# Query lots looked at one by one in the ring, six query sums in the long burst, and a two-input epsilon

## The chip, the cores and the metric

One Trainium2 chip, one core. The number that counts is device time in microseconds for one execution. The kernel before takes 1162.13 us (median of 3 runs, 1161.17 to 1162.33).

## The reference, cut to what matters

Agent attention, then a feed-forward layer with a cosine gate. 4 batches of 12480 tokens with 128 channels, 49 agents for each batch, float32 throughout.

```python
def sm(a, b):                                   # scaled, shifted softmax
    s = (a @ b.T) / sqrt(128)
    e = exp(s - s.max(-1))
    return e / (e.sum(-1) + 1e-9)
agent_v = sm(agents, k) @ v                     # 49 x 128 for each batch
x = sm(q, agents) @ agent_v                     # one row for each token
h = x @ w_in                                    # 2048 wide
out = (h * cos(h)) @ w_out
```

## The kernel before

Tokens are worked on in 52 query lots (NQ) of 960 tokens, 13 for each batch, laid out as 120 partitions x 8 rows (GT). For a lot the query weights are a 120 x 8 x 49 array: scores against the agents (TensorE), minus the maximum over 49 (a reduction and a subtraction), exponential (ScalarE), sum over 49, plus epsilon, reciprocal (VectorE), product with the reciprocal (GpSimd), transposition (TensorE) and a split into two parts (GpSimd).

The main loop has 832 steps, 16 for each lot (8 pairs of w_in columns x 2 halves of the lot). A step issues two matmuls `ph`, one ScalarE cosine `c`, one VectorE instruction `r` (the cosine minus one, times h), and, four steps later (LAG), two matmuls `po` that accumulate the output. The `ph` tiles come from a ring of three PSUM tiles of two banks each (ps_h): the matmuls of step n+3 wait until VectorE has read the tile of step n. There is one more PSUM tile for everything small (`one`) and one for the accumulator `po`.

Everything else is laid into these steps by two lists, `plan` (work ahead of the VectorE instruction of its step) and `post` (work behind it). Each engine runs its instructions in program order, so an instruction that waits holds up all behind it on its engine. Among this work are the next batch's key scores and running maximum (`scores`, `rank`), the split of its exponentials and values for TensorE (`split`, on GpSimd), its sums (`values`), and the query lots.

Sine and exponential are in different ScalarE tables, so exponentials are done in bursts (`burst`), with a table load ahead and behind. `pieces` lists the lots whose exponentials share a burst. There are three kinds:

- the long burst, at step 112 of batches 0 to 2 (T1): the key exponentials of the next batch in three parts, then the exponentials of six query lots. The scores of four further lots are made here too, two at a time, by two calls of `query_two`, each in one ring tile, one bank for each lot.
- the short bursts, at step 26 and at step 8 of batches 1 to 3: the exponentials of six or seven query lots, and one `query_two`.
- a last one of four lots at step 96 of batch 3, without `query_two`.

Behind its exponentials, a long burst sums the first SF lots on VectorE (`query_sum`), adds epsilon and takes the reciprocals (`query_inverse`), all in its own step. From four steps later (SM) it sums the others one in a step, and one step after the last sum adds epsilon and takes the reciprocals again. In the other bursts three lots are summed on VectorE (SD1) and the rest on GpSimd (`query_sums`).

`query_inverse` adds epsilon by `tensor_scalar_add` (EP = 0); the branch for EP = 1 is there already: `scalar_tensor_tensor(rz, rz, EPS, rz, op0=add, op1=max)`, which takes the maximum of rz + epsilon and rz. `rank` starts the running maximum of each batch by `tensor_copy`. All recorded instructions go through one wrapper, so the profile gives line 182 for nearly all; they are told apart by their tiles.

Of the kernel before, what the change touches and what calls it, by code (L numbers as in the profile page):

```python
# [9 lines left out]
F32 = mybir.dt.float32  # L10
# [5 lines left out]
AX = mybir.AxisListType  # L16
# [3 lines left out]
TT = 120  # L20
GT = 8
# [24 lines left out]
SH = 1  # L46
AD = 2
KB = 24
SF = 3
ST = 4  # L50
SD0 = 2
SD1 = 3
# [50 lines left out]
PO = 14  # L103
PK = 0
BM = 38
EP = 0
BZ = 12
TS = 1
VX = [5, 6, 7, 8]
# [35 lines left out]
def agent_attention_cos_ffn(ctx, tc, qT, kT, v, agT, w_in, w_out, outT):  # L145
    nc = tc.nc
    NB, _, N = qT.shape
    NA = agT.shape[2]
# [39 lines left out]
    pe, dve, act, pool = (Ordered(x) for x in (nc.tensor, nc.vector, nc.scalar, nc.gpsimd))  # L188
# [25 lines left out]
    def load(dst, src):  # L214
        ins = nc.sync.dma_start(dst, src)
        if pinned[0]:
            tc.keep_in_program_order(ins)

    def twice(x):

        return x.unsqueeze(1).to_broadcast([x.shape[0], 2, NA])
# [89 lines left out]
    class Agents:  # L311
# [50 lines left out]
        def rank(self, g):  # L362
            self.ranks = g + 1
            if g == 0:
                dve.tensor_copy(self.run, self.part(g))
            else:
                dve.tensor_max(self.run, self.run, self.part(g))

# [247 lines left out]
    with ExitStack() as pools:  # L616
        sb = pools.enter_context(tc.tile_pool(name="sb", bufs=2))
# [8 lines left out]
        def pair():  # L626
            return ps_h.tile([P, 2, 512], F32, name="ph")
# [4 lines left out]
        a = []  # L632
# [25 lines left out]
        e_of, rz_of = {}, {}  # L658
# [41 lines left out]
        def query_two(two, piece):  # L700

            ps = pair()[:TT]
            for j, n in enumerate(two):
                xt = sb.tile([P, GRP], F32, name="xt", bufs=XT)
                load(xt, qT[n // NG, :, n % NG * GRP:(n % NG + 1) * GRP])
                for t in range(GT):
                    pe.matmul(ps[:, j, t * NA:(t + 2) * NA].rearrange("p (x a) -> p x a", x=2) if WB else ps[:, j, t * NA:(t + 1) * NA],
                              xt[:, t * TT:(t + 1) * TT], twice(ag[:, n // NG, :]) if WB else ag[:, n // NG, :], start=True, stop=True)
            ps = ps[:, :, :GT * NA].rearrange("p j (t a) -> p j t a", a=NA)
            mx = sb.tile([TT, 2, GT], F32, name="mx3", bufs=2)  # L710
            dve.reduce_max(mx, ps, axis=AX.X)
            room(piece)
            i = piece.index(two[0])
            dve.tensor_sub(whole[piece][:, i * GT:(i + 2) * GT].rearrange("p (j t) a -> p j t a", j=2), ps,
                           mx.unsqueeze(3).to_broadcast([TT, 2, GT, NA]))

        whole = {}

        def room(piece):
            if piece in whole:  # L720
                return
            if OG and piece == pieces[-1]:
                e = ab[-1].s[:, :len(piece) * GT]
                rz = sb.tile([TT, len(piece) * GT], F32, name="rz3", bufs=1)
            else:
                e = sb.tile([P, PIECES * GT, NA], F32, name="e", bufs=EB)[:TT]
                rz = sb.tile([TT, PIECES * GT], F32, name="rz2", bufs=EB)
            whole[piece] = e
            for i, k in enumerate(piece):
                e_of[k], rz_of[k] = e[:, i * GT:(i + 1) * GT], rz[:, i * GT:(i + 1) * GT]  # L730
            e_of[piece], rz_of[piece] = e[:, :len(piece) * GT], rz[:, :len(piece) * GT]
# [22 lines left out]
        def query_inverse(piece, i, j):  # L754
            rz = rz_of[piece][:, i * GT:j * GT]
            if EP:
                dve.scalar_tensor_tensor(rz, rz, EPS, rz, op0=ALU.add, op1=ALU.max)
# [139 lines left out]
        piece = pieces[0]  # L897
# [11 lines left out]
        for g in range(NG):  # L909
# [6 lines left out]
            ps = pair()  # L916
# [88 lines left out]
        plan, post = Plan(), Plan()  # L1005
# [25 lines left out]
        def burst(n, piece, two=(), ab=None, also=()):  # L1031

            shut.update(range(n, n + SHUT))
            wide_at.update(range(n, n + SHUT + WX))
            for i in range(0, len(two), 2):
                post(n + i // 2 * BD, query_two, two[i:i + 2], piece_of[two[0]])
            if ab is not None:
                for g, k in lots:
                    post(n, pinned_exp, ab, g, k)
            post(n, query_exp, piece)  # L1040
            if also:
                post(n, query_exp, also)
                post(n + 12, query_sums, also, 0, len(also))
                post(n + 20, query_inverse, also, 0, len(also))
            s0 = SF if ab is not None else SD1
            for k in piece[:s0]:
                post(n, query_sum, k)
            post(n, query_inverse, piece, 0, s0)
            m = n + SM
            if ab is not None:  # L1050
                for k in piece[s0:]:
                    post(m, query_sum, k)
                    m += 1
                post(m, query_inverse, piece, s0, len(piece))
                return
            for i in range(s0, len(piece), ST):
                j = min(i + ST, len(piece))
                post(m, query_sums, piece, i, j)
                m += 1
            post(m + (SR if n < T3 + (NB - 1) * PER else SZ), query_inverse, piece, s0, len(piece))  # L1060
# [20 lines left out]
        late = [pieces[2 * b + 3] for b in range(NB - 1)] + [()]  # L1081
        spread_over(SA, S0 - SD, S0 - SD, [q_lot(n) for n in pieces[1]])
        burst(S0 + 2, pieces[1], early[0][:N0])
        for b in range(NB):
            o = b * PER
# [9 lines left out]
            if b == NB - 1:  # L1095
                spread_over(k0, go - 5, go - 1, [q_lot(n) for n in early[b][N2:]])
                burst(go, early[b])
                for c in range(DFF // 512):
                    if BZ >> c & 1:
                        post(go, big_late)  # L1100
                for i in range(FB):
                    post(go + FO, keep_warm)
                break
# [11 lines left out]
            for g in range(NG):  # L1115
                plan(k1 + 16 + SH * g, nxt.shift, g, 1, pool)
            burst(go, early[b], late[b][:N1], nxt)
            for g in range(0, NG, VP):
                at = go + V0 + (o + V1 - go - V0) * g / NG
# [7 lines left out]
            i = (b + 1) % 2  # L1127
# [11 lines left out]
        while queue or begun:  # L1139
# [4 lines left out]
            x = min(ready, key=lambda x: (x[2], x[1]))  # L1144
            if x is not begun:
                queue.remove(x)
            n, i, by, parts = x
# [17 lines left out]
        for n in range(NSTEP + LAG):  # L1165
# [3 lines left out]
            if n < NSTEP:  # L1169
                q, c, i = n // STEP, n // NP % NCH, n % NP  # L1170
# [31 lines left out]
            m = n - LAG  # L1202
            if m < 0:
                continue
            q, c, i = m // STEP, m // NP % NCH, m % NP
# [41 lines left out]
    with tc.If(far):  # L1247
        with ExitStack() as pools:
            sb = pools.enter_context(tc.tile_pool(name="gsb", bufs=2))
# [8 lines left out]
            p = sb.tile([TT, HT, 2 * HI], F32, name="p", bufs=1)  # L1258
# [121 lines left out]
```

## Time and profile before

| | |
|---|---|
| time of the runs shown | 1162.13 us, median (1161.17 to 1162.33) |
| the profiled execution | 1160.97 us; its span, first to last instruction, 1159.2 us |
| granted TensorE clock | 0.998 over the span |
| busy, share of the span | PE 97%, DVE 92%, ACT 84%, POOL 49% |
| chain that ended last | PE 62%, DVE 21%, ACT 11%, issue 4%, POOL 1% |
| DVE: `r`, whole tiles | 808 instructions, 891.4 us |
| DVE: reductions over two lots, `mx` from `ph` | 10 instructions, 9.7 us |
| DVE: sums `rz` of one lot | 36 instructions, 18.3 us |
| DVE: epsilon, 24 elements | 13 instructions, 6.0 us |

PE is TensorE's matmuls, DVE is VectorE, ACT is ScalarE, POOL is GpSimd. A busy share is over the whole span; a burst is a few microseconds in which other engines bound the work than in the steps around it. The chain of waits follows back from the last instruction, at each step to what released it.

### The profile page before, as it was taken

What the parts mean: (1) busy time and instruction counts of PE and PEld (TensorE: products, weight loads), DVE (VectorE), ACT (ScalarE), POOL (GpSimd) and SP (SyncE); (2) the same over time, 40 slices, a digit from 0 to 9 for tenths busy, and PEclk for the clock granted to TensorE, in tenths of its full rate; (3) what the DMA queues carried; (4) which work ended last, traced back from release to release, by engine and by line L of the source; (5) the groups of instructions that cost most, each with busy time, mean ns of one, the idle gap of its engine ahead of it and who ended that gap; (6) DMA issues with size and microseconds to landing.
All of it is one profiled execution on the core that took longest, in us unless ns stands there. A gap on an engine that the chain in (4) does not pass through costs nothing.

```text
span 1159.2 us, 17231 instructions
## 1 busy us (share of the span) xinstructions
PE 1118.7 (97%) x6075; PEld 924.1 (80%) x6075; DVE 1064.4 (92%) x1201; ACT 977.2 (84%) x1268; POOL 564.2 (49%) x726
## 2 busy tenths in 40 slices
PE   9989999999999999999999999999999999999996
PEld 8869888878887888877887888887888777767774
DVE  5888989999998999989999999998999899999996
ACT  3568877889889888898888887888988999999996
POOL 2013313678964122559893331366896455535551
PEclk9999999999999999999999999999999999999999
DMA  8734342143332232233331332224331100000001
GB/s 331 308 141 136 104 130 92 57 148 101 99 106 68 85 103 86 86 104 106 107 108 53 110 96 86 86 68 139 108 107 52 35 18 35 34 18 35 18 35 38
DMA packets 31631, 109.44 MB, mean 94 GB/s; under 512 B 3504, under 2 KB 4016, under 8 KB 31536
## 3 DMA queue, kind: packets, MB, share of 16 engines
q1 hardware_dynamic: 31392, 108.13, 28.7%
q8 instruction: 50, 0.82, 0.3%
q14 instruction: 45, 0.37, 0.1%
q10 hardware_dynamic: 144, 0.12, 0.0%
HBM read 82.68 MB, written 25.56 MB: 93 GB/s over the span
## 4 chain that ended last, share of the span: by engine, by line
PE 62%; DVE 21%; ACT 11%; issue 4%; POOL 1%; DMA 0%; ACTq 0%; DVEq 0%
PE ph L182 27%; PE po L182 23%; DVE r L182 15%; PE one L182 12%; ACT c L182 6%; DVE rz L182 2%; ACT osb L182 2%; DVE e L182 1%; DVE mx L182 1%; ACT p L182 1%; DVE sums L182 1%; ACT s L182 1%; ACT e L182 1%; ACT L182 1%; DVE s L182 1%
## 5 line engine op out<-in xcount | busy, mean ns | idle before, releaser
L182 DVE SCALAR_TENSOR_TENSOR r<-c,ph 128x960 fp32r<-128x960 f32 (+1 forms) x833 | 907.4, 1132 | 49.1 <-ACT c L182 41.8
L182 ACT ACTIVATE c<-ph 128x960 f32<-128x960 f32 x832 | 783.5, 977 | 132.8 <-PE ph L182 122.5
L182 PE MATMUL ph<-pT,a 113*128 113x480 f32 x1664 | 517.1, 392 | 16.3 <-DVE r L182 12.6
L182 PE MATMUL po<-r,w 128*128 128x480 f32 x1664 | 523.8, 396 | 5.6 <-ACT osb L182 5.3
L182 PEld LDWEIGHTS ph<-pT,a 113*128 113x128 f32 x1664 | 296.7, 189 | 123.0 <-DVE r L182 60.9
L182 PEld LDWEIGHTS po<-r,w 128*128 128x128 f32 x1664 | 291.8, 189 | 52.7 <-ACT osb L182 14.8
L182 POOL CAST pT<-p 49x480 fp32r<-49x480 f32 x102 | 59.2, 580 | 282.6 <-ACT p L182 279.8
L182 PEld LDWEIGHTS one<-ag,xt 128*120 128x120 f32 x1088 | 134.7, 184 | 11.3 <-DVE sums L182 1.5
L182 PE MATMUL one<-ag,xt 128*120 128x98 f32 x1088 | 134.2, 265 | 0.7 <-DVE b L182 0.4
L182 POOL TENSOR_TENSOR pT<-p,pT 49x480 fp32r<-49x480 f32 x102 | 124.1, 1217 | 8.2
L182 POOL TENSOR_TENSOR vh<-vt,vh 120x512 fp32r<-120x512 f32 x78 | 93.3, 1196 | 30.6 <-ACT vh L182 30.6
L182 POOL TENSOR_TENSOR p<-e,rz 120x392 f32<-120x392 f32 x51 | 43.5, 853 | 48.1 <-DVE rz L182 47.0
L182 PE MATMUL po<-pT,b 113*128 113x480 f32 x208 | 62.4, 381 | 0.0
L182 POOL TENSOR_TENSOR raw<-c,raw 128x480 f32<-128x480 f32 x23 | 28.3, 1229 | 70.0 <-ACT raw L182 69.9
L182 ACT COPY osb<-po 128x480 f32<-128x480 f32 x104 | 58.1, 559 | 2.2 <-PE po L182 2.2
L182 PEld LDWEIGHTS ph<-ag,xt 128*120 128x120 f32 x480 | 53.1, 188 | 7.5 <-DVE r L182 4.4
L182 PE MATMUL ph<-ag,xt 128*120 128x98 f32 x480 | 55.4, 272 | 3.1 <-DVE r L182 2.0
L182 POOL TENSOR_TENSOR e<-e,mx 120x392 f32<-120x392 f32 x26 | 21.9, 843 | 71.0 <-DVE mx L182 71.0
L182 PEld LDWEIGHTS one<-vh,eh 120*113 120x113 f32 x312 | 45.9, 177 | 8.2 <-POOL vh L182 2.5
L182 PE MATMUL one<-vh,eh 120*113 120x258 f32 x312 | 50.7, 284 | 1.4 <-DVE e L182 0.9
L182 POOL TENSOR_TENSOR eh<-s,eh 120x196 fp32r<-120x196 f32 x78 | 47.6, 610 | 6.3
L182 PEld LDWEIGHTS po<-pT,b 113*128 113x128 f32 x208 | 38.8, 188 | 6.0
(137 smaller groups left out, 725.4 us busy)
## 6 DMA issues: line engine op xcount, KB each, us to landing
xt<-qT SPq DMA_DIRECT2D x52, 480.0 KB, 3.5
outT<-osb SPq DMA_DIRECT2D x51, 480.0 KB, 2.8
xt<-kT SPq DMA_DIRECT2D x46, 480.0 KB, 3.7
vt<-v SPq DMA_DIRECT2D x43, 512.0 KB, 3.7
c<-kT SPq DMA_DIRECT2D x6, 480.0 KB, 6.9
vh<-v SPq DMA_DIRECT2D x5, 512.0 KB, 6.6
raw<-w_in SPq DMA_DIRECT2D x2, 512.0 KB, 6.5
a<-w_in SPq DMA_DIRECT2D x2, 512.0 KB, 5.7
```

What stands on the lines that cost most here:

```text
L182: ins = f(*args, **kw)
```

## The change

Three settings and two functions. `SF` goes from 3 to 6, so in a long burst all six query lots are summed in the burst's own step, with one epsilon and one reciprocal instruction for the six; the four later posts (three sums, one inverse) are gone. `query_two` makes the scores of one lot, then the maximum and the difference of that lot, then those of the other; the tile is still one for both, a bank for each. `EP` goes from 0 to 1, and `rank` starts with `tensor_max` of the part with itself in place of a copy.

```diff
-SF = 3
+SF = 6
...
-EP = 0
+EP = 1
...
             if g == 0:
-                dve.tensor_copy(self.run, self.part(g))
+                dve.tensor_max(self.run, self.part(g), self.part(g))
...
                 for t in range(GT):
                     pe.matmul(ps[:, j, t * NA:(t + 2) * NA].rearrange("p (x a) -> p x a", x=2) if WB else ps[:, j, t * NA:(t + 1) * NA],
                               xt[:, t * TT:(t + 1) * TT], twice(ag[:, n // NG, :]) if WB else ag[:, n // NG, :], start=True, stop=True)
-            ps = ps[:, :, :GT * NA].rearrange("p j (t a) -> p j t a", a=NA)
-            mx = sb.tile([TT, 2, GT], F32, name="mx3", bufs=2)
-            dve.reduce_max(mx, ps, axis=AX.X)
-            room(piece)
-            i = piece.index(two[0])
-            dve.tensor_sub(whole[piece][:, i * GT:(i + 2) * GT].rearrange("p (j t) a -> p j t a", j=2), ps,
-                           mx.unsqueeze(3).to_broadcast([TT, 2, GT, NA]))
+                x = ps[:, j, :GT * NA].rearrange("p (t a) -> p t a", a=NA)
+                mx = sb.tile([TT, GT], F32, name="mx3", bufs=4)
+                dve.reduce_max(mx, x, axis=AX.X)
+                room(piece)
+                dve.tensor_sub(e_of[n], x, mx.unsqueeze(2).to_broadcast([TT, GT, NA]))
...
-                post(m, query_inverse, piece, s0, len(piece))
+                if s0 < len(piece):
+                    post(m, query_inverse, piece, s0, len(piece))
```

## Rows read from the trace of the kernel before

**Rows 1.** The page: busy time of each engine, share of the span, instructions.
```profile
PE 1118.7 (97%) x6075; PEld 924.1 (80%) x6075; DVE 1064.4 (92%) x1201; ACT 977.2 (84%) x1268; POOL 564.2 (49%) x726
```

**Rows 2.** Busy engines by stretch, second long burst: PE, PEld, DVE, ACT, POOL, clock, DMA.
```profile
516.00:529.00 13.00, 11.29 (x52) 7.47 (x51) 12.83 (x17) 10.33 (x14) 11.88 (x16) 1.00 0.53 156
529.00:566.00 37.00, 36.62 (x184) 30.39 (x183) 36.39 (x38) 33.41 (x41) 31.52 (x46) 1.00 0.30 89
```

**Rows 3.** Timeline of DVE, second long burst: start, length, operation, [idle before].
```profile
511.97 0.97 DVE L182 TENSOR_REDUCE mx<-ph 120x16 f32<-120x784 f32 x1 [1.66 <-PE ph L182]
...
513.87 1.49 DVE L182 TENSOR_REDUCE rz<-e 120x8 f32<-120x392 f32 x3
515.39 0.18 DVE L182 TENSOR_SCALAR rz<-rz 120x24 f32<-120x24 f32 x1
...
516.10 1.16 DVE L182 SCALAR_TENSOR_TENSOR r<-c,ph 128x960 fp32r<-128x960 f32 x1 [0.20 <-ACT c L182]
517.17 0.56 DVE L182 TENSOR_REDUCE mx<-one 120x8 f32<-120x392 f32 x1
...
518.25 3.27 DVE L182 SCALAR_TENSOR_TENSOR r<-c,ph 128x960 fp32r<-128x960 f32 x3
...
526.37 0.86 DVE L182 TENSOR_SCALAR rz<-rz 120x24 f32<-120x24 f32 x1
...
527.48 3.22 DVE L182 SCALAR_TENSOR_TENSOR r<-c,ph 128x960 fp32r<-128x960 f32 x3
```

**Rows 4.** Timeline of ACT, the same burst.
```profile
511.17 2.62 ACT L182 ACTIVATE e<-e 120x392 f32<-120x392 f32 x6
...
515.10 0.97 ACT L182 ACTIVATE c<-ph 128x960 f32<-128x960 f32 x1
```

**Rows 5.** Timeline of PE, the same burst.
```profile
528.63 0.70 PE L182 MATMUL ph<-pT,a 113*128 113x480 f32 x2 [0.49 <-DVE r L182]
```

**Rows 6.** Groups of DVE instructions by form: busy us, mean ns, idle before.
```profile
L182 DVE RECIPROCAL rz<-rz 120x24 f32<-120x24 f32 x13 | 3.9, 303 | 0.4
...
L182 DVE COPY run<-s 120x392 f32<-120x392 f32 x4 | 2.2, 538 | 7.4 <-ACT s L182 7.4
```

**Rows 7.** Timelines of PE, DVE and POOL, first long burst.
```profile
233.96 1.92 PE L182 MATMUL ph<-ag,xt 128*120 128x98 f32 x16 [0.69 <-DMA xt<-qT]
...
239.77 1.09 DVE L182 SCALAR_TENSOR_TENSOR r<-c,ph 128x960 fp32r<-128x960 f32 x1
...
240.04 1.20 POOL L182 TENSOR_TENSOR vh<-vt,vh 120x512 fp32r<-120x512 f32 x1 [7.42 <-ACT vh L182]
```

**Rows 8.** Timelines of PE, DVE, ACT and POOL, short burst of batch 1.
```profile
366.09 3.60 PE L182 MATMUL ph<-ag,xt 128*120 128x98 f32 x32 [0.36 <-DVE r L182]
...
375.62 0.70 PE L182 MATMUL ph<-pT,a 113*128 113x480 f32 x2 [0.70 <-DVE r L182]
...
373.22 1.00 DVE L182 TENSOR_SCALAR rz<-rz 120x24 f32<-120x24 f32 x1
...
372.41 1.83 ACT L182 ACTIVATE c<-ph 128x960 f32<-128x960 f32 x2
...
371.24 1.86 POOL L182 TENSOR_TENSOR raw<-e 120x768 f32<-120x768 f32 x1 [4.45 <-ACT e L182]
373.18 2.45 POOL L182 TENSOR_TENSOR raw<-raw 120x384 f32<-120x384 f32 x4
```

**Rows 9.** Timelines of DVE and POOL: a running maximum beside a GpSimd product.
```profile
395.46 0.66 DVE L182 TENSOR_TENSOR run<-run,s 120x392 f32<-120x392 f32 x1
...
394.85 0.84 POOL L182 TENSOR_TENSOR p<-e,rz 120x392 f32<-120x392 f32 x1
```

**Rows 10.** Timeline of DVE, last burst.
```profile
1025.07 1.50 DVE L182 TENSOR_REDUCE rz<-e 120x8 f32<-120x392 f32 x3 [0.45 <-ACT e L182]
...
1038.55 0.79 DVE L182 TENSOR_SCALAR rz<-rz 120x8 f32<-120x8 f32 x1
```

**Rows 11.** Timeline of ACT, last burst.
```profile
1024.51 1.79 ACT L182 ACTIVATE e<-e 120x392 f32<-120x392 f32 x4
```

## The prediction

> **What bounds the kernel now.** I read the page first: PE is busy 97% of the span, DVE 92%, ACT 84% [rows 1]. With three engines this close an average says little, so I cut the span into stretches and looked around each burst. The stretch behind the second long burst stands apart: in 516 to 529 us DVE is busy 12.83 of 13 us and PE 11.29, while in the 37 us after it PE is busy 36.62 [rows 2]. So PE sets the pace nearly everywhere, and DVE does for some 13 us behind each of the three long bursts. The timeline of PE confirms it: its last idle time there, at 528.63, is ended by DVE's `r` [rows 5]. The chain of waits shows the same for some 10 us behind the short bursts of batches 1 and 2, where PE sits idle 0.70 us for `r` [rows 8]. Work taken off DVE is worth something in these stretches, up to PE's idle time in them, and nearly nothing elsewhere.
>
> **Six sums in the long burst.** Removed behind each long burst: three single sums, one epsilon, one reciprocal. A sum costs DVE 0.47 us of pace: three in a row last 1.49, one of them 0.55 with its tail, so (1.49 - 0.55) / 2 [rows 3, 10]. Three are 1.41. From the second epsilon to the next `r` it is 527.48 - 526.37 = 1.11 [rows 3]. Together 2.52 us.
>
> Added in the burst itself: `r` cannot start before the sums end. In the second burst the scores of the fourth lot are there at 511.97 [rows 3]. Looked at alone, that lot needs a maximum and a difference over 392 elements, together 518.25 - 517.17 = 1.08 for the same pair elsewhere [rows 3], so sums begin at 513.05. The exponentials start at 511.17 and six take 2.62, some 0.42 each [rows 4]; each is ready before its sum. Six sums last 5 x 0.47 + 0.55, with the hand-over 2.93: epsilon at 515.98. I take 0.24 for epsilon on 48 elements in the two-input form, near the 0.18 that the old form lasts with 24 [rows 3]. The reciprocal takes 303 ns with 24 elements [rows 6]; with 48 it lies between that and 606, I take 450, of which DVE is held about 0.37, since its tail lies under the next operation. `r` starts at 516.59, against 516.10 before: 0.49 later. The cosine is not what it waits for, ready at 515.10 + 0.97 [rows 4]. In the first long burst the fourth lot's scores come late, since its load does [rows 7]: the lot is there at 233.96 + 1.92 = 235.9, epsilon comes at 239.93 and `r` at 240.54, against 239.77 [rows 7], 0.77 later. The third goes like the second.
>
> DVE gains 2.52 - 0.49 = 2.0 us in the second and third burst and 1.75 in the first. PE cannot follow all the way: its idle time in the stretch is 1.7 us [rows 2], and a little of it, at the start, waits on the now later `r`. Following PE's instructions one by one behind the new times of `r`, I get 1.6, 1.55 and 1.3 us: 4.45 together. Bounds: 0.5 for each, if another engine takes over (below), and 2.0.
>
> In the first burst a tie is near. GpSimd takes up an operation of 1.20 us at 240.04 [rows 7], and epsilon falls at 239.93. If it comes behind, it can be held as the long epsilons of the trace are [rows 3, 8], by up to 1.2 us, and the first burst gives about 0.2. I leave this in the range.
>
> **One lot at a time.** Each `query_two` has one reduction and one difference more. DVE holds about 2.16 us for two lots in place of about 1.95, but now begins 1.8 us earlier (half of the 3.60 that 32 matmuls last [rows 8]), in time in which DVE was idle for PE (1.66 us in the row at 511.97 [rows 3]). Behind the second lot's scores only 1.08 is left. In the long bursts this is used up above. In the short burst of batch 1 the second lot is there at 366.09 + 3.60 = 369.7 [rows 8]; sums from 370.81, epsilon at 370.81 + 2 x 0.47 + 0.55 + 0.03 = 372.33. Before, epsilon came at 373.22 and lasted 1.00 [rows 8]. It had come just behind the start of a GpSimd operation at 373.18, and lasted until about the end of the first of that group. The new epsilon falls into the GpSimd operation ahead of that one, which runs from 371.24 to 373.10 [rows 8]. If held, it ends at about 373.15; then reciprocal, and `r` at 373.40. The cosine is ready at 372.41 + about 0.97 = 373.38 anyway [rows 8]. Before, `r` came at 373.22 + 1.00 + 0.25 = 374.47. So 1.05 us earlier for DVE; PE has 0.70 idle for it at 375.62 [rows 8] and about 0.3 more a few microseconds on: I take 1.0, bounds 0.5 and 1.1. Batch 2 repeats it: 2.0 together. At the short bursts of batch 0 (step 26) and batch 3 `r` waits for the cosine, or for nearly as long: nothing taken, 0.2 at most. What covers the two extra instructions is the second lot's matmuls; without that cover they would cost 0.2 for each of the 10 calls.
>
> **Epsilon by two inputs, maximum for copy.** The trace has no two-input epsilon on so few elements. What it shows of waiting: a running maximum with two SBUF inputs began at 395.46, while GpSimd's product ran from 394.85 to 395.69, and lasted 0.66 [rows 9], against 0.56 for a reduction over as many elements elsewhere [rows 3]. It ended 0.43 behind the product, about the time that 392 elements stream in. So an operation with two inputs is held behind GpSimd too. I take nothing for this edit. Bounds: -0.1 per epsilon, if the two-input form is longer, and, if it were never held, 0.6 at the last burst (0.79 at 1038.55 [rows 10] against 0.18 [rows 3]) and some 0.5 at one more of the kind: a gain of 1.1. The copy that starts a running maximum lasts 538 ns on the mean of four [rows 6], a maximum 0.56 to 0.66 [rows 9]: 0.1 more for each, in steps where DVE has that much to spare, so I take nothing; bounds 0 and 0.4.
>
> The Trainium skill ("SBUF — State Buffer", section "SBUF: two separate sides") says that VectorE and GpSimd take a port pair exclusively, a VectorE operation with two SBUF inputs as well, against a GpSimd operation that reads SBUF. By that rule this edit saves nothing; by the thought that only the one-input form is held it would save the 1.1 us. The trace agrees with the rule, by the 0.66 above.
>
> **Sum.** 4.45 + 2.0 = 6.45 us. The profiled execution took 1160.97, 1.2 below the median of the runs, which is 1162.13; 1160.97 - 6.45 = 1154.5, and against the median 1155.7.
>
> **The rivals.**
>
> *GpSimd takes over behind the long burst.* It is busy 11.88 of the 13 us there and 31.52 of the next 37 [rows 2]; it splits the values that PE multiplies. Of its 1.1 us idle about 0.66 is its wait at the start. If PE ran up against it, each long burst would give about 0.5, all 1.5, with the short ones 3.5: 1158.6. Against it: the wait that ends last for PE in that stretch is on `r` [rows 5], and the splits are done a microsecond or more ahead of their use.
>
> *The two-input form is not held.* Then 6.45 + 1.1 = 7.55: 1154.6. Against it: rows 9.
>
> *The ring tile keeps an order between its lots.* The first lot is now read before the second lot's matmuls in program order, in the same tile. If these waited for the read to end, the second lot would come at 366.09 + 1.8, plus DVE's still running `r` and the 1.08 of reading, plus 1.8: 371.0 in place of 369.7, 1.3 later. A long burst would have it twice, about 2.4. Three long and three short bursts: 11.1 us lost against 6.45 gained, 1166.8; it is slower from about 0.65 a call. Against it: in the last burst the first sum begins at 1025.07, while the exponentials of other lots of the same tile, issued ahead of it, run until 1026.30 [rows 10, 11], so order goes by the part of a tile that is touched, not by the tile.
>
> *Nothing moves.* The time in the bursts is given back at once, within 0.2% (2.3 us, about what a measurement of this kernel can tell from no change): 1161 to 1162. Against it: PE's 36.62 of 37 behind the burst [rows 2], an engine with nothing to give back to.
>
> **How the numbers follow.** Forecast, gains of 5 to 8.6 us: 0.55, its time 1155.7. GpSimd taking over or the first burst's tie lost, 2.3 to 5: 0.18. Two-input form not held: 0.12. Nothing moves: 0.08. An order in the ring: 0.07. Faster is 0.55 + 0.18 + 0.12 = 0.85, same 0.08, slower 0.07. The range holds the first three but for their ends: from 1153.0 (every DVE gain of 2.0 kept, 1.1 in the short bursts, some of the 1.1 of epsilon) to 1159.6.
>
> **What would show it.** Right: three single sums and the second epsilon gone behind each long burst; six sums in a row, `r` 0.5 us later behind the cosine there, and PE's idle time for `r` near 528 gone; in the short bursts of batches 1 and 2 `r` starts as the cosine ends, with maxima of 120x8 while the second lot's matmuls run. Epsilon still lasts up to 1 us where GpSimd runs. Wrong: matmuls of a second lot that wait for DVE; PE waiting for POOL's `vh` or `eh` behind the long burst; an epsilon of over 1 us at 240 us; every epsilon at 0.2.

## The result and the profile after

The kernel after takes 1169.77 us (median of 4 runs, 1169.35 to 1170.44), the kernel before 1161.94 beside it: 1.0068 times as long, 95% interval 1.0056 to 1.0081. It is 7.8 us slower; the forecast was 6.4 faster, and the range, 1153.0 to 1159.6, misses by 10.

Busy time on the page is nearly that of [rows 1]: no engine has more work to do.

```profile
PE 1115.2 (96%) x6075; PEld 924.3 (79%) x6075; DVE 1064.7 (91%) x1215; ACT 977.7 (84%) x1268; POOL 564.4 (48%) x726
```

What changed is a wait. PE's groups by form (busy, mean ns, then idle time ahead and who ended it): first the row of after, then that of before.

```profile
L182 PE MATMUL ph<-ag,xt 128*120 128x98 f32 x480 | 55.9, 270 | 15.8 <-DVE e L182 13.5 <-DVE r L182 2.0 <-DMA xt<-kT 0.4
```
```profile
L182 PE MATMUL ph<-ag,xt 128*120 128x98 f32 x480 | 55.4, 272 | 3.1 <-DVE r L182 2.0 <-DMA xt<-qT 0.8
```

13.5 us of idle time, ended by DVE's `e`, which is the difference of a query lot, in ten calls of `query_two`: 1.35 a call on the mean, 1.26 to 1.36 in nine of them and 1.67 at step 26. The second long burst shows where it lies. PE of before, then of after:

```profile
504.61 7.32 PE L182 MATMUL ph<-ag,xt 128*120 128x98 f32 x64 [0.31 <-DVE r L182]
...
517.31 0.70 PE L182 MATMUL ph<-pT,a 113*128 113x480 f32 x2 [0.17 <-DVE r L182]
```

```profile
509.06 1.92 PE L182 MATMUL ph<-ag,xt 128*120 128x98 f32 x16 [0.29 <-DVE r L182]
512.33 3.60 PE L182 MATMUL ph<-ag,xt 128*120 128x98 f32 x32 [1.35 <-DVE e L182]
517.19 1.92 PE L182 MATMUL ph<-ag,xt 128*120 128x98 f32 x16 [1.26 <-DVE e L182]
...
524.97 0.71 PE L182 MATMUL ph<-pT,a 113*128 113x480 f32 x2 [0.65 <-DVE r L182]
```

And DVE of after there, which answers to [rows 3]:

```profile
511.05 0.56 DVE L182 TENSOR_REDUCE mx<-ph 120x8 f32<-120x392 f32 x1
511.71 0.57 DVE L182 TENSOR_TENSOR e<-ph,mx 120x392 f32<-120x392 f32 x1
514.29 0.57 DVE L182 TENSOR_REDUCE mx<-ph 120x8 f32<-120x392 f32 x1 [2.01 <-PE ph L182]
...
519.15 0.57 DVE L182 TENSOR_REDUCE mx<-ph 120x8 f32<-120x392 f32 x1 [2.01 <-PE ph L182]
519.75 0.57 DVE L182 TENSOR_TENSOR e<-ph,mx 120x392 f32<-120x392 f32 x1
520.23 2.89 DVE L182 TENSOR_REDUCE rz<-e 120x8 f32<-120x392 f32 x6
523.16 0.26 DVE L182 SCALAR_TENSOR_TENSOR rz<-rz 120x48 f32<-120x48 f32 x1
523.45 0.45 DVE L182 RECIPROCAL rz<-rz 120x48 f32<-120x48 f32 x1
523.82 1.09 DVE L182 SCALAR_TENSOR_TENSOR r<-c,ph 128x960 fp32r<-128x960 f32 x1
```

The sixteen matmuls of a second lot begin only when DVE has finished with the first, though they write another bank; then DVE stands idle for them. The two engines take turns where, before, the 64 matmuls of four lots ran on without a break. From the first lot's matmuls to `r` it is 523.82 - 509.06 = 14.76 us here and 516.10 - 504.61 = 11.49 before; 2.89 - 1.49 = 1.40 of the difference is the three sums that now lie in the burst. The 32 matmuls at 512.33 are the second lot of one call and the first of the next: those two, in different ring tiles, do follow each other without a wait.

The short burst of batch 1 has the same, beside [rows 8]. PE and DVE of after, then the `r` of before:

```profile
370.12 1.92 PE L182 MATMUL ph<-ag,xt 128*120 128x98 f32 x16 [0.36 <-DVE r L182]
373.40 1.92 PE L182 MATMUL ph<-ag,xt 128*120 128x98 f32 x16 [1.35 <-DVE e L182]
```
```profile
377.96 0.30 DVE L182 SCALAR_TENSOR_TENSOR rz<-rz 120x24 f32<-120x24 f32 x1
378.29 0.30 DVE L182 RECIPROCAL rz<-rz 120x24 f32<-120x24 f32 x1
378.51 2.15 DVE L182 SCALAR_TENSOR_TENSOR r<-c,ph 128x960 fp32r<-128x960 f32 x2
```
```profile
374.48 2.15 DVE L182 SCALAR_TENSOR_TENSOR r<-c,ph 128x960 fp32r<-128x960 f32 x2
```

What DVE does in the burst is over 8.39 us after the first lot's matmuls begin (378.51 - 370.12), as it was before: 374.48 - 366.09 = 8.39, with an epsilon that lasted 1.00 [rows 8] where it lasts 0.30 now. The turn-taking eats what the shorter epsilon gives, and PE's idle time is no longer ahead of `r` (0.70 us before), but ahead of the second lot (1.35).

Behind the long burst the windows of after, 13 and 37 us from `r` on as in [rows 2] (busy PE, PEld, DVE, ACT, POOL, clock, DMA share, GB/s):

```profile
524.00:537.00 13.00, 11.89 (x61) 9.27 (x60) 12.96 (x15) 10.54 (x14) 10.28 (x14) 1.00 0.49 152
537.00:574.00 37.00, 36.34 (x182) 29.95 (x181) 35.89 (x38) 32.90 (x42) 32.84 (x47) 1.00 0.33 98
```

PE's idle time in the first is 1.1 us where it was 1.7: part of what the forecast meant to win there is won, though 0.3 of it is idle again in the second window, and it is less than what the burst itself lost.

By stage (from the sine table load behind the named burst to the next exponential table load on ScalarE, profiled executions; the runs e2 to e10 are described below), in us; the columns behind "before" are differences from it:

| stage behind | before | after | six sums alone (e2) | own tiles (e5) | three sums, own tiles (e6) | own tiles, no epsilon (e9) | five sums, own tiles (e10) |
|---|---|---|---|---|---|---|---|
| step 26 | 114.77 | +1.16 | -0.01 | 0.00 | +0.02 | 0.00 | 0.00 |
| long 1 | 129.56 | +1.25 | +0.15 | +2.71 | -0.08 | -1.61 | -0.54 |
| short, batch 1 | 134.22 | +0.43 | -0.02 | -1.10 | -1.15 | -1.12 | -1.13 |
| long 2 | 129.47 | +1.39 | +0.37 | -1.11 | +0.02 | -1.43 | -1.30 |
| short, batch 2 | 134.16 | +0.46 | +0.03 | -1.08 | -1.05 | -1.08 | -1.08 |
| long 3 | 129.44 | +1.48 | +1.73 | -1.16 | +0.07 | -1.26 | -1.28 |
| short, batch 3 | 99.14 | +0.91 | +0.03 | -0.08 | -0.07 | -0.10 | -0.06 |

Two entries hold a stretch at a lower TensorE clock besides: long 3 of e2 and long 1 of e5.

The seven stages of after add up to 7.1 us. Its work ahead of the first of them also ended 1.6 us later than in the profile of before (115.58 against 113.95); that start varies: it ended at 117.13 in the profile of e8, whose time equals that of before.

### The profile page after: what moved, and what is told of

Read it like the earlier page. It is cut to its first block, busy times and chain, and to the rows that moved or that the text cites. A ratio compares the mean times of both kernels' runs of the same rounds, so it can differ in the third digit from the quotient of the medians.

```text
span 1167.5 us, 17255 instructions
## 1 busy us (share of the span) xinstructions
PE 1115.2 (96%) x6075; PEld 924.3 (79%) x6075; DVE 1064.7 (91%) x1215; ACT 977.7 (84%) x1268; POOL 564.4 (48%) x726
## 4 chain that ended last, share of the span: by engine, by line
PE 61%; DVE 19%; ACT 10%; issue 4%; POOL 3%; DMA 1%; SPq 0%; ACTq 0%; DVEq 0%; POOLq 0%
PE ph L182 26%; PE po L182 23%; DVE r L182 14%; PE one L182 12%; ACT c L182 7%; ACT osb L182 2%; DVE rz L182 1%; POOL pT L182 1%; DVE e L182 1%; ACT p L182 1%; DVE mx L182 1%; POOL vh L182 1%; DVE sums L182 1%; DMA vh<-v 1%; POOL eh L182 0%
## 5 line engine op out<-in xcount | busy, mean ns | idle before, releaser
L182 PEld LDWEIGHTS one<-ag,xt 128*120 128x120 f32 x1088 | 134.7, 184 | 11.4 <-DVE sums L182 1.5
L182 PE MATMUL ph<-ag,xt 128*120 128x98 f32 x480 | 55.9, 270 | 15.8 <-DVE e L182 13.5
```

Of the source, the lines that this page charges most:

```text
L182: ins = f(*args, **kw)
```

## The experiments

Three theories at first. A: the ring tile keeps an order between its lots, as in the rival of that name. B: it is the six sums, which make `r` late. C: the epsilon or maximum edit costs.

**e1, the lots one by one alone** (before, with the new loop of `query_two`; SF, EP and copy as before).

> The kernel before with query_two of the changed kernel alone (three sums in the long burst and the old epsilon stay). Theory A, the tile keeps an order: the second lot's matmuls wait for the difference of the first, some 1.3 us in each of the 10 calls; at the first burst the changed kernel lost 1.15 us, in which nothing else of the change acts. Long bursts have two calls and lose some 2.6 us each, short ones 0.5 to 1.2: 10 to 12 us in all, ratio 1.009 to 1.010, about 1173 us. Theory B, the six sums in the burst are what costs: this kernel is as fast as before or 1 to 2 us faster (1160 to 1162). Theory C, the late load of the values at the start of the changed kernel (1.6 us) belongs to the edits of epsilon and copy: here the start is as before.

1173.5 us, ratio 1.0093 (1.0074 to 1.0112). This edit alone costs more than the whole change, as A has it. Its long bursts are 2.2 to 2.5 us longer than before, those of after 1.25 to 1.5: even here the six sums are worth 1.0 a burst. The rest of its distance to after lies behind step 26, where the profile has 1.6 us more than after: PE's wait is as long there in both (1.68 and 1.67), but in e1 the clock is lower behind it. PE of e1, its window (busy PE, PEld, DVE, ACT, POOL, granted clock, DMA share, GB/s), and PE of after:

```profile
113.34 2.77 PE L182 MATMUL ph<-ag,xt 128*120 128x98 f32 x16 [1.68 <-DVE e L182]
```
```profile
114.00:118.00 4.00, 4.00 (x21) 3.71 (x20) 1.82 (x4) 2.46 (x5) 0.45 (x1) 0.57 0.32 83
```
```profile
113.94 1.92 PE L182 MATMUL ph<-ag,xt 128*120 128x98 f32 x16 [1.67 <-DVE e L182]
```

**e2, six sums alone.**

```diff
-SF = 3
+SF = 6
...
+                if s0 < len(piece):
...
```

> The kernel before with six sums in the long burst alone. Theory A: nothing waits in the ring; each long burst gains 1.3 to 1.6 us behind it, 4 to 4.8 us in all, about 1157.5 us, ratio 0.996. r in the long burst starts some 0.9 us later behind the cosine than in the kernel before (1.43 us of sums more, of which the cosine's wait hid a part). Theory B: slower, since r starts later in each long burst: 1165 to 1170.

1164.7 us, ratio 1.0023 (1.0010 to 1.0036): a miss. By itself this edit gives nothing; it costs. The second long burst of e2, on DVE, PE and POOL:

```profile
515.93 2.89 DVE L182 TENSOR_REDUCE rz<-e 120x8 f32<-120x392 f32 x6
518.86 0.95 DVE L182 TENSOR_SCALAR rz<-rz 120x48 f32<-120x48 f32 x1
519.84 0.45 DVE L182 RECIPROCAL rz<-rz 120x48 f32<-120x48 f32 x1
520.21 1.09 DVE L182 SCALAR_TENSOR_TENSOR r<-c,ph 128x960 fp32r<-128x960 f32 x1
```
```profile
521.36 0.70 PE L182 MATMUL ph<-pT,a 113*128 113x480 f32 x2 [2.08 <-DVE r L182]
522.52 0.71 PE L182 MATMUL one<-vh,eh 120*113 120x258 f32 x4 [0.46 <-POOL vh L182]
```
```profile
518.57 1.19 POOL L182 TENSOR_TENSOR vh<-vt,vh 120x512 fp32r<-120x512 f32 x1 [7.43 <-ACT vh L182]
```

The sums begin behind a look at both lots at once (0.97 + 0.97, where the forecast had one lot). So the epsilon falls 0.29 us behind the start of GpSimd's first operation and is held for most of it. PE waits 2.08 us for `r`, where it waited 0.17 before: `r` is put off by the three further sums, 1.40 us, and by the longer epsilon, 0.77 (0.95 against 0.18). The gain behind is eaten. Behind the third long burst the granted clock is also lower for a while, and that stage is 1.73 us longer, the other two 0.15 and 0.37.

**e3, the kernel after with the old `query_two`** (six sums, two-input epsilon, maximum).

> The changed kernel with query_two as it was before: six sums, two-input epsilon, maximum for copy. Theory A: faster than before by 4 to 5 us, like the six sums alone, about 1157.5; the edit of epsilon adds nothing (0 to 0.5 us either way). If the two-input epsilon were not held by GpSimd: some 1 us faster than the six sums alone. Theory B: 1165 to 1170. Theory C: its start (first sine table load) lies 1.6 us later than in the kernel before; otherwise at the same time within 0.3 us.

1167.32 us, ratio 1.0034 (1.0014 to 1.0054): a miss again, for the reason of e2. Its epsilon of the second long burst lasts 1.02 us, PE waits 2.14, and in this profile the clock is lower behind all three long bursts, where in that of e2 it is behind one.

**e4, both lots' matmuls first, then the two looks** (after, the loop of `query_two` cut in two).

> The changed kernel, with the matmuls of both lots issued ahead of the first look; the looks stay one by one. Theory A: PE never waits for DVE in query_two. If reads are ordered by the part of the tile that they touch, DVE begins on the first lot while the second is computed, and it is what was forecast for the changed kernel: 1154.5 to 1157. If reads too are ordered by the tile, DVE begins behind the second lot's matmuls, with 2.16 us of looking in place of 1.95: 1157.5 to 1158.5. Theory B: 1167 to 1170.

1167.25 us, ratio 1.0042 (1.0027 to 1.0058): a miss that tells more than a hit would have. PE's wait for `e` is gone, and yet DVE does not look at the first lot any earlier. Short burst of batch 1, PE and DVE of e4:

```profile
367.69 3.60 PE L182 MATMUL ph<-ag,xt 128*120 128x98 f32 x32 [0.36 <-DVE r L182]
```
```profile
371.33 0.57 DVE L182 TENSOR_REDUCE mx<-ph 120x8 f32<-120x392 f32 x1 [1.56 <-PE ph L182]
```

367.69 + 3.60 = 371.29: the look at the first lot waits for the last matmul of the second. So the order holds both ways, as if by the tile. That is theory T, tried next. The time itself is that of e2 and e3 once more: six sums behind both looks, epsilons of 0.73 to 0.89 us, PE's waits for `r` of 1.95 to 2.33 in the long bursts, and a lower clock behind two of them.

**e5, a ring tile for each lot**, all else as after.

```diff
-            ps = pair()[:TT]
             for j, n in enumerate(two):
+                ps = pair()[:TT]
```

> The kernel after, with a ring tile of its own for each lot of a `query_two` (one line moved; the order of matmuls, looks and differences is unchanged). Theory T (order goes by the whole ring tile, in both directions: the second lot's matmuls wait for the difference of the first, and a look at the first lot waits for the last matmul of the second): both waits go. The row of PE's lot matmuls shows no wait on DVE's `e`, the first maximum of 120x8 begins about 1.9 us after its lot's matmuls began, and `r` of the short burst of batch 1 comes about 1.0 us earlier against the cosine than in the run with both lots' matmuls first; 7 us less than the kernel after for ten calls, and a little for the long bursts: 1159 to 1163 us. Rival U (the look of DVE itself costs the time, four operations in place of two): no more than 1 us better than both lots' matmuls first, 1166 to 1168. Rival V (six sums with their epsilon keep `r` late whatever the looks do): the waits go, PE still waits about 1.2 us for `r` in the long bursts, 1164 to 1166.

1158.35 us, ratio 0.9960 (0.9946 to 0.9974): 3 us faster than before by the medians (nearer 5 by the ratio) and 11 faster than after, by moving one line. Second long burst, PE and DVE of e5:

```profile
509.23 5.28 PE L182 MATMUL ph<-ag,xt 128*120 128x98 f32 x48 [0.29 <-DVE r L182]
514.95 1.89 PE L182 MATMUL ph<-ag,xt 128*120 128x98 f32 x16 [0.43 <-DMA xt<-qT]
...
522.64 0.70 PE L182 MATMUL ph<-pT,a 113*128 113x480 f32 x2 [0.59 <-DVE r L182]
```
```profile
511.22 0.56 DVE L182 TENSOR_REDUCE mx<-ph 120x8 f32<-120x392 f32 x1
...
520.88 0.21 DVE L182 SCALAR_TENSOR_TENSOR rz<-rz 120x48 f32<-120x48 f32 x1
```

Three lots' matmuls run on without a break while DVE looks at the first; the fourth waits 0.43 us for its load and for no engine. T stands, U falls, and V with it, since PE waits 0.59 us for `r` here. But its runs spread from 1155.58 to 1161.77, and the first long burst is 2.7 us longer than before. There, on DVE, POOL and PE of e5:

```profile
243.08 1.24 DVE L182 SCALAR_TENSOR_TENSOR rz<-rz 120x48 f32<-120x48 f32 x1
```
```profile
243.06 1.19 POOL L182 TENSOR_TENSOR vh<-vt,vh 120x512 fp32r<-120x512 f32 x1 [7.42 <-ACT vh L182]
```
```profile
245.87 0.70 PE L182 MATMUL ph<-pT,a 113*128 113x480 f32 x2 [1.62 <-DVE r L182]
...
249.60 1.01 PE L182 MATMUL po<-r,w 128*128 128x480 f32 x2
```

The tie that the forecast left in its range is lost, by 0.02 us: the epsilon lasts 1.24 where it lasts 0.21 in the second burst. PE stands idle 1.62 us, and then its granted clock is at the lower level, as the window of e5 shows (the last three columns are granted clock, DMA share and GB/s):

```profile
247.00:253.00 6.00, 5.97 (x19) 5.32 (x20) 4.93 (x6) 3.04 (x4) 3.43 (x6) 0.50 0.58 169
```

**e6, the same with three sums, old epsilon and copy.**

> The kernel before, with the lots looked at one by one in ring tiles of their own; three sums and the old epsilon and copy stay. Theory T: `r` about 1.0 us earlier in the short bursts of batches 1 and 2, and up to 0.5 in each long burst: 1158 to 1160 us, faster than before by 2 to 4. Rival U: 1162 to 1165, since eight operations more for two pairs cost DVE about 0.2 a call and no wait is shortened. If the long bursts alone keep what the short ones gain, 1161 to 1162.

1159.79 us, ratio 0.9984 (0.9975 to 0.9993). All of its gain is in the short bursts (-1.15 and -1.05); the long ones give nothing with three sums.

**e7, the kernel before once more.**

> The kernel before, unchanged, as a second build: what a difference of nothing looks like, and a second profile of it. If the late start of the five changed profiles (their first sine table comes 1.0 to 1.8 us later than in the profile of before) belongs to the profile of before and not to the changes, this one begins its first sine table at 66 to 67 us too, with a span of 1160 to 1161; if the start is the changes', it begins at 65.1 with a span of about 1159. Time 1161 to 1162.5 either way.

1161.30 us, ratio 1.0002 (0.9990 to 1.0013). Every stage comes within 0.2 us of the first profile, and its start is early too (114.22). The two profiles of before both start early; e10, with nearly the whole change, starts as early (114.04), and e8, with the epsilon alone, latest of all (117.13). Part of it is a load: PE waits 1.48 us for the values (`vh` from `v`) at 38.78 us in e8 and 1.39 at 37.27 in after, and not at all in before and e10. What delays the load stays open, but e8 and e10 speak against the change.

**e8, the two-input epsilon alone.**

```diff
-EP = 0
+EP = 1
```

> The kernel before with the epsilon as a two-input operation, nothing else (the copy that starts the running maximum stays). My prediction took nothing for it: 1161 to 1163. Rival W (the run with old looks, six sums, epsilon and maximum came 2.6 us behind the one with six sums alone, so the two-input epsilon or the maximum costs time of its own): 1163.5 to 1165 if it is the epsilon, no change if it is the maximum.

1162.02 us, ratio 1.0005 (0.9993 to 1.0016): nothing, as forecast. C falls as far as the epsilon goes.

**e9, own tiles, no epsilon in the long bursts.**

```diff
-        def query_inverse(piece, i, j):
+        def query_inverse(piece, i, j, add=True):
             rz = rz_of[piece][:, i * GT:j * GT]
-            if EP:
+            if not add:
+                pass
+            elif EP:
...
-            post(n, query_inverse, piece, 0, s0)
+            post(n, query_inverse, piece, 0, s0, ab is None)
```

> Lots in ring tiles of their own, six sums, and the epsilon left out in the three long bursts (a part of the computation left out: 1e-9 is not added to those sums). In the run with own tiles the epsilon of the first long burst began 0.02 us behind GpSimd's first operation, lasted 1.24 us where the second burst's lasted 0.21, PE then stood idle 1.62 us, and its granted clock was at half for some 6 us behind that. Theory D (that held epsilon is what still costs: 1.0 us of wait in the first burst, and the clock with it): `r` of the first burst 1.2 us earlier, PE's idle time there 0.4 to 0.7, no stretch at a lower clock before the end, 1154.5 to 1156.5 us and a spread of under 2. Rival E (the wait is only handed on, to the cosine or to GpSimd's `vh`): 1157.5 to 1159.5, as with the epsilon, and as spread.

1155.51 us, ratio 0.9942 (0.9930 to 0.9955), all five runs within 0.6. PE's wait in the first long burst is 0.37. That is what D says, but in this profile the fourth lot's scores were also there earlier in the first burst, against the table load, than in e5, and the sums end 0.68 us ahead of GpSimd's operation, where in e5 the epsilon, which follows the sums at once, began 0.02 behind it. DVE and POOL of e9:

```profile
237.84 2.89 DVE L182 TENSOR_REDUCE rz<-e 120x8 f32<-120x392 f32 x6
```
```profile
241.41 1.19 POOL L182 TENSOR_TENSOR vh<-vt,vh 120x512 fp32r<-120x512 f32 x1 [7.42 <-ACT vh L182]
```

An epsilon of 0.21 us would have passed there too. So e9 alone does not decide; e10 does.

**e10, own tiles, five sums in the burst.**

```diff
-SF = 6
+SF = 5
```

> Lots in ring tiles of their own, five sums in the burst, the sixth with an epsilon and a reciprocal of its own behind it. Theory D: the epsilon comes 0.47 us earlier, ahead of GpSimd's operation in every long burst, PE waits under 0.6 us there and keeps its clock; behind the burst DVE has 0.47 + 1.1 us more to do, of which PE feels up to 0.5 a burst: 1155 to 1157. Rival E: 1158 to 1160.

1155.56 us, ratio 0.9943 (0.9930 to 0.9956), with the whole computation: with e14 the fastest complete version, 6 to 7 us ahead of before and 14 ahead of after. First long burst, DVE and POOL of e10:

```profile
239.77 0.20 DVE L182 SCALAR_TENSOR_TENSOR rz<-rz 120x40 f32<-120x40 f32 x1
```
```profile
240.13 1.20 POOL L182 TENSOR_TENSOR vh<-vt,vh 120x512 fp32r<-120x512 f32 x1 [7.42 <-ACT vh L182]
```

One sum fewer, and the epsilon is through 0.16 us ahead of GpSimd; a sixth sum of 0.47 us would have brought it behind. PE waits less than 0.5 us there and its clock stays up. D stands: what e5 lost was the held epsilon and the clock behind it.

**e11, e5 once more.**

> The run with own tiles once more, unchanged, beside its two variants: 1155.5 to 1162 us, median 1157 to 1159; the profile shows whether the lower clock behind the first long burst comes again. By theory D a run with a mean clock of 0.998 is near 1156 and one of 0.995 near 1161.5.

1157.69 us, ratio 0.9960 (0.9948 to 0.9972). The epsilon is held again (1.24), PE waits 1.63, but this time the clock stays up, on PE and by window of e11:

```profile
243.46 0.70 PE L182 MATMUL ph<-pT,a 113*128 113x480 f32 x2 [1.63 <-DVE r L182]
```
```profile
244.60:250.60 6.00, 5.97 (x32) 4.84 (x33) 6.00 (x7) 4.75 (x7) 4.64 (x7) 1.00 0.58 169
```

The stage is +0.24 here and +2.71 in e5: the lower clock is worth 2.5 us, the held epsilon some 1.4 by itself (+0.24 against -1.21 and -1.05 in the other two bursts). The clock does not make the whole spread: the six times here run from 1155.76 to 1159.46, all with a mean clock of 0.997 or 0.998, against what D expected.

**e12, own tiles, GpSimd rounds the first value split.**

```diff
-            if VA and (2 * g + k) % VA == 0:
+            if VA and (2 * g + k) % VA == 1:
```

> Lots in ring tiles of their own, six sums, and the first of each three value splits rounded by GpSimd instead of ScalarE, the second by ScalarE: GpSimd need not wait 7.4 us in the long burst for ScalarE's rounding. Theory F (GpSimd's late start is what keeps the long bursts from giving the 1.55 us that I forecast, where they gave 1.1): GpSimd begins its `vh` some 5 us earlier, PE's waits on `vh` behind the burst go, 0.3 to 0.5 us more for each burst: 1156 to 1157.5 if the clock holds. Against it: GpSimd then runs beside the epsilon in all three bursts, which is held by up to 1.2 us in each, and beside the sums: 1159 to 1163.

1157.30 us, ratio 0.9965 (0.9953 to 0.9977). The time is as F has it, the reason is not. GpSimd does one operation earlier, and then waits 5.29 us for ScalarE all the same; the long bursts give 1.14, 1.14 and 1.11, no more than in e5. The first did better than in e5 and e11, with its epsilon (240.71) ahead of GpSimd (241.05): the fourth lot's matmuls waited 0.49 us for their load, where in e5 they waited 0.85. F falls.

**e13, after with narrow score matmuls** (49 columns each, none shared).

```diff
-WB = 1
+WB = 0
```

> The kernel after, with the score matmuls of `query_two` written 49 columns wide in place of 98, so that no two of them touch the same columns. If the ring tile as a whole keeps the order, the second lot's matmuls still wait for DVE's `e` by 1.0 to 1.5 us a call (1.35 and 1.26 in the second long burst of the kernel after). If the overlapping columns do, that wait is gone and the first maximum runs beside the second lot's matmuls. The time itself also moves with the narrower matmuls and decides nothing.

One run, 1192.5 us. PE of e13, second long burst:

```profile
518.79 1.88 PE L182 MATMUL ph<-ag,xt 128*120 128x49 f32 x16 [0.31 <-DVE r L182]
522.07 5.83 PE L182 MATMUL ph<-ag,xt 128*120 128x49 f32 x32 [1.40 <-DVE e L182]
529.16 3.44 PE L182 MATMUL ph<-ag,xt 128*120 128x49 f32 x16 [1.26 <-DVE e L182]
```

The same two waits: it is not the overlapping columns.

**e14, e10 with the old epsilon and copy.**

> Lots in ring tiles of their own and five sums, with the one-input epsilon and the copy of the kernel before. If these two edits do nothing here, as the run with the epsilon alone says: 1155 to 1156.5 us, the same as with them. If the two-input form is held less: 0.5 to 1 more, 1156 to 1157; if the maximum costs (four of them, up to 0.35 us each): 1154.5 to 1155.5.

1155.73 us, ratio 0.9947 (0.9934 to 0.9961), as e10. These two edits neither give nor take; the rest of C falls.

## Why the prediction was wrong

**The step that failed is the one on an order in the ring.** The forecast set it as a rival at 0.07, "1166.8; it is slower from about 0.65 a call", against "order goes by the part of a tile that is touched, not by the tile". It is what happened: PE waits 1.35 us a call on the mean, 13.5 in ten calls, where the rival had 11.1 us in all for nine; undoing it gains 11.4 (1169.77 to 1158.35). The forecast's overlap, a first lot looked at while the second lot's matmuls run, did not take place. It had priced the loss of that cover at 0.2 a call, DVE's extra work; what is lost is PE's time too, since each engine stands idle while the other works. What was argued against it came from an SBUF tile [rows 10, 11], written and read by slices; the tile in question is in PSUM, and no row of before showed one read by a lot while the other lot was written, since the old code never did that. The evidence was of another kind of tile, and I gave it the weight of the same kind. e4, e5 and e13 show the order: by the ring tile, in both directions, and not by columns that two matmuls share.

The Trainium skill ("PSUM — Partial Sum Buffer", section "The four PSUM rules") says that what a first matmul of a group clears is one bank and no other. By that rule alone two lots in two banks would need no order, which would leave the program's bookkeeping of tiles as the source of the waits of 1.26 to 1.67 us. e5 agrees, and so does the profile, which finds who ended a wait by semaphore events and names DVE's `e`; but no run took the order away within one tile, so that much is argued and not shown.

**One lot at a time: right, once the lots are apart.** Forecast 1.0 us in each short burst of batches 1 and 2, nothing in those of batches 0 and 3: with own tiles it is 1.10 and 1.08 (e5), 1.15 and 1.05 (e6), and 0.0 and 0.1 in the others. In the kernel after the turn-taking swallows it: +0.43 and +0.46.

**Six sums in the long burst: the right sign, but only on the back of that step, and a size too large.** The forecast let the sums begin behind one lot's look; with two (e2, e3) or with looks in turn (after) they begin later. With own tiles, six sums and the epsilon in place, a burst whose epsilon is not held gives 1.05 to 1.21 us (e5, e11, e12), for a forecast of 1.3 to 1.6. Only where the epsilon is left out do the three give 1.61, 1.43 and 1.26, together 4.30, for a forecast of 4.45 (e9). That the time of e9, 1155.51, and of e10 with five sums, 1155.56, is the forecast's 1155.7 is in part luck: neither is the kernel that was forecast. With six sums and the epsilon the stages give 5.6 us where the first burst's epsilon was not held (e12) and 4.3 where it was and the clock stayed up (e11), for 6.45. So the sum was near, but high, for a kernel one line away from the one that was changed.

**The tie at the first long burst** went the bad way where it could (e5, e11: 0.02 us behind GpSimd), and cost more than the range had for it: the burst lost 0.24 us where 0.2 of gain was left, with the clock up (e11), and 2.7 with the clock down (e5), which the forecast left out.

**Epsilon by two inputs: nothing, as forecast.** e8 and e14 say so; it is held behind GpSimd as the one-input form is (1.24 us in e5, 0.95 for the old form in e2). The Trainium skill's rule cited in the prediction ("SBUF — State Buffer", section "SBUF: two separate sides") agrees with the 1.24 of the two-input form. **GpSimd taking over** was no cause by itself: e12 moved its work and gained nothing in the bursts. The forecast's ground against this rival was put too high, though: the splits are not "a microsecond or more ahead of their use". Behind the second long burst of before the first `vh` ends at 516.66 + 1.19 = 517.85 us, and the matmuls that read `vh` begin at 518.48.

**Of the signs named ahead**, "matmuls of a second lot that wait for DVE" is the one that came.

Open: why the load is late at the start of some profiles; and whether PSUM tiles always keep such an order, or only those of this ring, and whether the kind of memory is what sets them apart from the SBUF tile (no other tile was tried).

## What to carry to other kernels

When two engines are to overlap on parts of one buffer, look in the trace for a place where that very kind of buffer is already shared so; if there is none, give each part a tile of its own, or price the loss of all overlap as the likely case. An edit that frees time on one engine is worth measuring again after the wait next to it is gone: six sums were a loss in e2 and worth 1.1 to 1.2 us in the two bursts of e5 whose epsilon was not held. A short operation just behind the start of a long one on GpSimd can cost the long one's length (1.24 us for 0.21 in e5); try shifting it by one instruction, as e10 did.

## What the runs showed of the hardware

**The clock.** In the profiles of before, after and e1 to e12 there are 42 long bursts. In 11 of them PE stood idle for 1.6 to 2.4 us waiting for `r` (three each in e2, e3 and e4, the first of e5 and of e11); in 7 of these the granted clock was then at the lower level, 1.2 GHz, for some microseconds of full work, pairs of matmuls lasting 1.01 us in place of 0.60. In none of the 31 others, with waits for `r` of up to 0.65 us, did it fall in the 10 us after the first `r`; six of these, of after and e1, have two waits of 1.26 to 1.36 us for `e` each. Outside the long bursts, but for the last microseconds of each run, it fell once, behind the wait of 1.68 us at step 26 of e1, and not behind the 1.67 there in after. That is an association over these runs; the wait was not varied by itself.

**Narrow matmuls.** Sixteen of 49 columns last 1.88 us, sixteen of 98 last 1.92. Nothing is saved, and in the one run of e13 the mean clock of the whole run is 0.969, where it is 0.997 in after, with half the clock for parts of all seven bursts that have a `query_two`. By window of e13, the first long burst (its clock is the 0.66):

```profile
232.00:245.00 13.00, 10.06 (x56) 9.37 (x56) 6.24 (x9) 11.01 (x13) 0.95 (x2) 0.66 0.35 105
```

It is 23 us slower than after; how much of that the clock makes was not separated.
